# Two interleaved attention and MLP layers: residual rows and the probability spread issued from SyncE, and softmax's second half one PV step sooner

## The chip, the cores and the metric

The kernel runs on one core of one Trainium2 chip. The metric is the device time of one execution in microseconds (us). A quoted time is the median of several executions. "Span" is the length of the profiled execution; events inside it are given in us from its start. For the kernel before, that was one more execution, of 1328.15 us, 3.5 us above the median of the timed ones; for every other kernel it is one of the timed ones. Kernels are compared only within the same rounds.

## The reference

Two identical layers run one after the other. A layer is a dilated sliding-window attention followed by an MLP over the tokens, each with a residual and a layernorm in front. Everything is in bf16, with S = 2048 tokens, D = 1024, 32 heads of 32, a window of W = 8 positions two apart, and F = 3584.

```python
def _A_ref(x, wqkv, wo):                       # attention
    q, k, v = ...                              # x @ wqkv, split in 32 heads of 32
    idx = pos[:, None] - arange(8)[None] * 2   # 8 earlier positions, two apart
    logits = einsum("bhsd,bhswd->bhsw", q, k[idx]) * scale     # masked where idx < 0
    attn = softmax(logits)
    return einsum("bhsw,bhswd->bhsd", attn, v[idx]) @ wo
def _B_ref(x, w1, b1, w2, b2):                 # MLP over the tokens
    u = gelu(einsum("bsd,sf->bdf", layernorm(x), w1) + b1)
    return (einsum("bdf,fs->bds", u, w2) + b2).transpose
x = A_x
for _ in range(2):
    x = x + _A_ref(layernorm(x), A_wqkv, A_wo)
    x = x + _B_ref(layernorm(x), B_w1, B_b1, B_w2, B_b2)
```

## The kernel before

Positions two apart never mix in the attention, so the tokens fall into two classes of 1024. Per layer the attention runs in four blocks (n = 0 to 3, two per class). VectorE multiplies q with shifted k (`T`), TensorE sums over the head's channels with a selection matrix (`sc`), and softmax follows on VectorE and ScalarE. The probabilities `Pb` are then needed on all partitions of a head, so they are written to DRAM (`pd`, 256 KB) and read back with every row repeated eight times (`pb`, two reads of 1 MB). This is the "spread". VectorE multiplies `pb` with shifted v (the PV step). TensorE never waits for all that as long as other matmuls (projections, pieces of the MLP) can be woven in between.

The parts that matter here (cuts marked with `...`):

```python
# softmax, second half: normalise, write to DRAM, read back spread
nc.vector.tensor_tensor(out=Pb[:], in0=L[:], in1=m4[:, 1:2, :].to_broadcast([P, W, TB]), op=ALU.mult)
base = self.pd(n)[0, 0]
dst = bass.AP(base.tensor, base.offset, [(W * TB, 4 * SB), (4 * SB * W * TB, CH), (1, W * TB)])
nc.gpsimd.dma_start(out=dst, in_=Pb[:].rearrange("p u t -> p (u t)"))
self.spread(n)
...
def spread(self, n):
    for hf in range(2):
        pb = pbp.tile([P, 4, W, TB], BF16, name="pb", tag="pb")       # two buffers in all
        base = self.pd(n)[4 * hf, 0]
        src = bass.AP(base.tensor, base.offset, [(4 * SB * W * TB, CH), (0, P // CH), (1, 4 * W * TB)])
        nc.gpsimd.dma_start(out=pb[:].rearrange("p b u t -> p (b u t)"), in_=src)
...
# weights: all from SyncE
nc.sync.dma_start(out=t, in_=src)                                     # wq, wv: 512 KB each
...
# residual rows, 256 KB each
nc.gpsimd.dma_start(out=xrs[-1][:], in_=res[len(xrs) - 1])            # xr, for the output projection
nc.gpsimd.dma_start(out=xs[:], in_=src[c][i * P:(i + 1) * P, :])      # xs, for the second matmul of the MLP
...
nc.gpsimd.dma_start(out=dst_v[i], in_=xn[:])                          # xa, the attention's result, written
```

## Time and profile before

| | |
|---|---|
| time | 1324.73 us, median of 3 (1324.02 to 1324.88) |
| TensorE busy | 1275.1 of 1326.4 us |
| idle gaps of TensorE of over 0.3 us, summed | 40.0 us |
| stretches at half clock after such gaps | 30.6 us long, so some 15 us lost |
| `pb` read, issue to landing | 11.9 us (median of 16) |

These lines are from the page of the kernel before: busy time by engine, the granted TensorE clock in 40 slices of the span (tenths of full speed), the two DMA queues that matter (q0 is GpSimd's, q1 SyncE's; packets, MB, share of the DMA engines' time), and three kinds of transfer (count, KB each, median us to landing).

```profile
PE 1275.1 (96%) x6164; PEld 577.1 (44%) x6284; DVE 683.5 (52%) x861; ACT 439.8 (33%) x740; POOL 95.7 (7%) x230
...
PEclk9998999999999999999998999999899999999999
...
q1 hardware_dynamic: 224432, 116.67, 32.8%
q0 software_dynamic: 14368, 54.29, 14.6%
...
pb<-pd POOLq DMA_DIRECT2D x16, 1024.0 KB, 11.9
...
xs<-xa POOLq DMA_DIRECT2D x32, 256.0 KB, 3.7
wv<-in_A_wqkv_dram SPq DMA_DIRECT2D x14, 512.0 KB, 6.5
```

TensorE is busy 96% of the time, so only its gaps can be won. What ended its waits (the list of waits of TensorE before: us in total, times, longest):

```profile
PE sc L444 <- DVE T L439: 10.8, 4, 5.0
PE ps L622 <- DVE oT L506: 9.5, 3, 6.3
PE ps L681 <- DVE xo L686: 7.2, 1, 7.2
PE ps L622 <- DMA wo<-in_A_wo_dram: 3.4, 2, 2.9
PE ps L655 <- DVE xn L628: 2.1, 1, 2.1
```

With the letters that the prediction uses: A (102 us into the span, 5.0 us) and B (213 us, 4.4 us) are in the first line, C (301 to 303 us, 3.1 us) and F (946 us, 6.3 us) make the second, E (717 us, 7.2 us) is the third, H (197 us, 2.9 us) is in the fourth, D (340 us, 2.1 us) is the fifth. E is worth a look, because the change aims at it: the `xs` rows were issued at 704.8 us, behind the spread in GpSimd's program, and took 11.4 us (the instructions of tile `xs`, before, in this window; the issue line has count, duration, first and last start):

```profile
L672 POOL DMA_DIRECT2D xs<-xa x2: 543/547/551, 704.8 to 718.6; - x2
...
DMA to landing us min/median/max: 4.1/7.8/11.4
```

The weight load `wv` at 132.6 us lands in 3.7 us, though the spread of block 1 was issued 0.8 us after it, at 133.4 us (tiles `wv` and `pb`, before, 125 to 150 us):

```profile
L387 SPq DMA_DIRECT2D wv<-in_A_wqkv_dram x1: 368/368/368, 132.6 to 132.6; - x1
...
DMA to landing us min/median/max: 3.7/3.7/3.7
```

```profile
L482 POOL DMA_DIRECT2D pb<-pd x2: 513/513/513, 133.4 to 133.9; - x2
```

### The profile page before, as it was taken

What the parts mean: (1) busy time and instruction counts of PE and PEld (TensorE: products, weight loads), DVE (VectorE), ACT (ScalarE), POOL (GpSimd) and SP (SyncE); (2) the same over time, 40 slices, a digit from 0 to 9 for tenths busy, and PEclk for the clock granted to TensorE, in tenths of its full rate; (3) what the DMA queues carried; (4) which work ended last, traced back from release to release, by engine and by line L of the source; (5) the groups of instructions that cost most, each with busy time, mean ns of one, the idle gap of its engine ahead of it and who ended that gap; (6) DMA issues with size and microseconds to landing.
All of it is one profiled execution on the core that took longest, in us unless ns stands there. A gap on an engine that the chain in (4) does not pass through costs nothing.

```text
span 1326.4 us, 15310 instructions
## 1 busy us (share of the span) xinstructions
PE 1275.1 (96%) x6164; PEld 577.1 (44%) x6284; DVE 683.5 (52%) x861; ACT 439.8 (33%) x740; POOL 95.7 (7%) x230
## 2 busy tenths in 40 slices
PE   8999998999999999999997999999799999999999
PEld 4343433443444444444443444444344444444444
DVE  6879998989102323234796734878950033111111
ACT  6844445731313420024434424475122144000000
POOL 3000000101000000000001010011010000000000
PEclk9998999999999999999998999999899999999999
DMA  9751545553432248864658662438162232334331
GB/s 256 168 125 56 128 114 140 168 145 96 132 87 74 74 139 215 214 171 117 159 158 223 196 176 64 95 108 234 44 202 64 70 90 72 117 95 137 118 117 60
DMA packets 239448, 173.00 MB, mean 130 GB/s; under 512 B 32208, under 2 KB 227152, under 8 KB 237328
## 3 DMA queue, kind: packets, MB, share of 16 engines
q1 hardware_dynamic: 224432, 116.67, 32.8%
q0 software_dynamic: 14368, 54.29, 14.6%
q8 instruction: 49, 0.80, 0.3%
q10 hardware_dynamic: 576, 1.05, 0.2%
q14 instruction: 23, 0.19, 0.0%
HBM read 146.81 MB, written 18.87 MB: 125 GB/s over the span
## 4 chain that ended last, share of the span: by engine, by line
PE 64%; DVE 6%; DMA 4%; issue 1%; ACT 0%; POOL 0%; DVEq 0%
PE ps L681 27%; PE ps L655 22%; PE ps L409 11%; PE ps L622 3%; DVE pr L500 2%; DVE pr L504 1%; PE sc L444 1%; DMA xs<-xa 1%; DMA wq<-in_A_wqkv_dram 1%; DMA pb<-pd 1%; DMA xa<-xn 1%; DMA hT<-hb 0%; DVE xn L628 0%; DVE T L439 0%; DVE xn L625 0%
## 5 line engine op out<-in xcount | busy, mean ns | idle before, releaser
L681 PE MATMUL ps<-g,w 128*128 128x512 bf16 (+1 forms) x1786 | 389.8, 377 | 9.4 <-DVE xo L686 7.2
L655 PE MATMUL ps<-h,w 128*128 128x512 bf16 x1758 | 388.1, 380 | 5.3 <-DVE xn L628 2.1
L681 PEld LDWEIGHTS <-w 128*128 128x128 bf16 x1820 | 178.1, 98 | 219.4 <-issue 13.3
L655 PEld LDWEIGHTS <-w 128*128 128x128 bf16 x1792 | 175.8, 98 | 217.0 <-issue 7.2
L409 PE MATMUL ps<-hT,wq 128*128 128x512 bf16 (+1 forms) x1084 | 241.7, 376 | 4.6 <-DMA hT<-hb 1.6
L686 DVE SCALAR_TENSOR_TENSOR xo<-ps,b_sb,xs 128x512 bf16<-128x512 f32 (+1 forms) x65 | 45.6, 737 | 255.2 <-PE ps L681 239.6
L666 DVE TENSOR_TENSOR tmp<-ps,g 128x512 f32<-128x512 f32 x80 | 55.3, 692 | 229.0 <-PE ps L655 225.9
L439 DVE TENSOR_TENSOR T<-q,k 128x4096 bf16<-128x4096 bf16 x60 | 136.0, 2287 | 65.2 <-ACT q L413 55.5
L409 PEld LDWEIGHTS <-wq 128*128 128x128 bf16 x1112 | 108.8, 100 | 133.5 <-issue 13.6
L504 DVE TENSOR_TENSOR pr<-pr 128x2048 bf16<-128x2048 bf16 (+1 forms) x128 | 119.2, 947 | 0.1
L622 PE MATMUL ps<-wo,oT 128*128 128x512 bf16 x375 | 92.3, 384 | 13.7 <-DVE oT L506 9.5
L409 PE MATMUL ps<-hT,wv 128*128 128x512 bf16 x436 | 102.2, 384 | 0.9 <-issue 0.4
L416 ACT CAST k<-ps 128x1024 bf16<-128x1024 f32 x60 | 60.8, 1016 | 77.8 <-PE ps L409 76.5
L500 DVE TENSOR_TENSOR pr<-pb,v 128x2048 bf16<-128x2048 bf16 x64 | 75.8, 1214 | 19.4 <-DMA pb<-pd 15.4
L667 ACT ACTIVATE g<-tmp,b_sb 128x512 bf16<-128x512 f32 x80 | 57.7, 721 | 82.1 <-DVE tmp L666 82.1
L500 DVE TENSOR_TENSOR pr<-pb,g 128x2048 bf16<-128x2048 bf16 x64 | 76.2, 1214 | 11.1 <-DMA pb<-pd 11.1
L409 PEld LDWEIGHTS <-wv 128*128 128x128 bf16 x448 | 48.8, 112 | 51.8 <-issue 8.7
L661 ACT CAST g<-ps 128x512 bf16<-128x512 f32 x80 | 45.6, 589 | 70.3 <-PE ps L655 66.8
L192 ACT ACTIVATE ln<-mv,eps 128x1 f32<-128x1 f32 x37 | 10.9, 294 | 165.0 <-DVE mv L201 157.4
L622 PEld LDWEIGHTS <-oT 128*128 128x128 bf16 x384 | 37.2, 99 | 62.8 <-DVE oT L506 10.7
L413 ACT CAST q<-ps 128x512 bf16<-128x512 f32 x60 | 35.0, 585 | 52.3 <-PE ps L409 51.2
L416 ACT CAST g<-ps 128x1024 bf16<-128x1024 f32 x36 | 36.5, 1017 | 41.1 <-PE ps L409 41.1
(94 smaller groups left out, 633.8 us busy)
## 6 DMA issues: line engine op xcount, KB each, us to landing
w<-in_B_w_dram SPq DMA_DIRECT2D x96, 448.0 KB, 3.7
w<-in_B_w_dram SPq DMA_DIRECT2D x56, 512.0 KB, 4.3
wq<-in_A_wqkv_dram SPq DMA_DIRECT2D x38, 512.0 KB, 4.0
pb<-pd POOLq DMA_DIRECT2D x16, 1024.0 KB, 11.9
wo<-in_A_wo_dram SPq DMA_DIRECT2D x16, 512.0 KB, 4.0
xa<-xn POOLq DMA_DIRECT2D x32, 256.0 KB, 3.4
xs<-xa POOLq DMA_DIRECT2D x32, 256.0 KB, 3.7
wv<-in_A_wqkv_dram SPq DMA_DIRECT2D x14, 512.0 KB, 6.5
```

What stands on the lines that cost most here:

```text
L409: nc.tensor.matmul(ps[:, lo:hi], lhsT=cols, rhs=self.hT[c][hf][:, kt, lo:hi], start=(kt == 0), stop=(kt == KD - 1))
L416: nc.scalar.copy(out=window(buf, 0, PADK + hf * HT, [(KW + 1, 2), (1, HT)]), in_=ps[:].unsqueeze(1).to_broadcast([P, 2, HT]))
L439: nc.vector.tensor_tensor(out=T[:], in0=q.unsqueeze(1).to_broadcast([P, 4, SC]), in1=window(k, par, 2, [(2, 4), (1, SC)]), op=ALU.mult)
L500: nc.vector.tensor_tensor(out=pr[:, :, u, :], in0=pb[:, :, u, :], in1=window(self.v_of(c, dt), par, 2 + hf * HT, [(TB, 4), (2, 4), (1, TB) ...
L504: nc.vector.tensor_tensor(out=pr[:, :, 0:wd, :], in0=pr[:, :, 0:wd, :], in1=pr[:, :, wd:2 * wd, :], op=ALU.add)
L622: nc.tensor.matmul(ps[:], lhsT=at_.oT[c][kt][:, i * P:(i + 1) * P], rhs=wo_t[n][kt // 4][:, kt % 4, :], start=(kt == 0), stop=(kt == KD - 1))
L655: nc.tensor.matmul(ps[:], lhsT=wt[c][:, i, fl * P:(fl + 1) * P], rhs=h2[c][i // 4][:, i % 4, dc * 512:(dc + 1) * 512], start=(k == 0), sto ...
L661: nc.scalar.copy(out=gs, in_=ps[:])
L666: nc.vector.tensor_tensor(out=tmp[:], in0=ps[:], in1=gs, op=ALU.add)
L667: nc.scalar.activation(out=gs, in_=tmp[:], func=ACT.Gelu_apprx_tanh, bias=b1_sb[:, ft:ft + 1])
L681: nc.tensor.matmul(ps[:, 0:xc.stop - xc.start], lhsT=w2t[n][:, ft % HF, c::DIL], rhs=g[ft // GF][:, ft % GF, xc], start=(ft == 0), stop=(f ...
L686: nc.vector.scalar_tensor_tensor(out=xo[:, xc], in0=ps[:, 0:xc.stop - xc.start], scalar=b2_sb[:, i, c:c + 1], in1=xs[:, xc], op0=ALU.add, ...
```

## The change

The intent: GpSimd issues the spread, the residual rows and the result writes, and each waits behind the others in its program. Taking the rows and the spread to SyncE should free the `xa` writes (gap B) and the rows (gap E), and bring the spread forward a little. Softmax's second half is put ahead of one PV unit, so that `Pb` is ready sooner. The diff, complete but for context lines:

```diff
-            nc.gpsimd.dma_start(out=dst, in_=Pb[:].rearrange("p u t -> p (u t)"))
+            nc.sync.dma_start(out=dst, in_=Pb[:].rearrange("p u t -> p (u t)"))
             self.spread(n)
...
-                nc.gpsimd.dma_start(out=pb[:].rearrange("p b u t -> p (b u t)"), in_=src)
-        def pv(self, n, half, hf):
+                nc.sync.dma_start(out=pb[:].rearrange("p b u t -> p (b u t)"), in_=src)
+        def pv(self, n, half, hf, dqs=(0, 1)):
...
-            for dq in (2 * half, 2 * half + 1):
+            for dq in (2 * half + x for x in dqs):
...
                     if pv:
-                        yield from self.pv(n - 1, half, 0)
+                        yield from self.pv(n - 1, half, 0, (0,))
                     if half:
                         yield from self.softmax_back(n)
                     if pv:
+                        yield from self.pv(n - 1, half, 0, (1,))
                         yield from self.pv(n - 1, half, 1)
...
-                nc.gpsimd.dma_start(out=xrs[-1][:], in_=res[len(xrs) - 1])
+                nc.sync.dma_start(out=xrs[-1][:], in_=res[len(xrs) - 1])
...
-        nc.gpsimd.dma_start(out=xs[:], in_=src[c][i * P:(i + 1) * P, :])
+        nc.sync.dma_start(out=xs[:], in_=src[c][i * P:(i + 1) * P, :])
```

Below, "spread" means the `pd` and `pb` lines, "rows" the `xr` and `xs` lines, "order" the softmax lines.

## The prediction

> **What bounds it now.** TensorE. Page: PE 1275.1 of 1326.4 us busy; the chain of waits is 64% PE. What can be won is PE's idle time: gaps in the timeline add up to 40 us, and the clock record falls to 0.5 for 3.4 or 6.8 us after most gaps of over about 2 us (101, 213, 302, 340, 715, 944 us), another 15 us. By the wait list and the chain:
> - A, 102 us, 5.0: products T late, VectorE having idled 7.1 us for pb<-pd
> - H, 197 us, 2.9: wo landed 6.3 us after issue
> - B, 213 us, 4.4: VectorE waited 5.0 us for xa<-xn, behind the spread (+10.9 us)
> - C/D, 301-340 us, 5.3: last PV, then xa<-xn
> - E, 717 us, 7.2: xs<-xa, behind the spread on GpSimd's queue (+11.5 us)
> - F, 946 us, 6.3: last spread (pd 4.4 us, pb 8.3 us), then PV.
>
> **What the change does.** Issues leave GpSimd for SyncE, so xr, xs and both spread legs share one in-order queue with the weights.
>
> *Cheaper.* Per spread: no 0.3 us wake-up of GpSimd per leg, slightly earlier first byte (packet records: 1.2 us after issue for GpSimd's, 1.0 for SyncE's): 1 to 1.5 us. The rate should stay: the two pb reads (2.1 MB) take about 10.5 us, in 8 KB packets of 0.55 us, which no issuer changes. xa writes no longer stand behind pb: B's wait mostly goes.
>
> *Softmax.* The instruction order shows that Pb moves by only about one VectorE instruction (1.1 us), as the scheduler interleaved it already; only the last block moves by five (3.4 us). In each layer one group of 8 matmuls (1.7 us of filling) slips behind the output projection, so C and F must win more than that.
>
> *Dearer.* The Trainium skill, "DMA: Bandwidth & Descriptors", section "Queues, rings and completion order", says a ring is consumed in order while different rings alternate by packet. The trace agrees: xr issued behind pb on GpSimd's queue lands with it (+12.3 us), while a weight load on SyncE's queue got through in 6.7 us. Weights issued behind pb will now wait for all of it. By landing against first use: the wv load at 132.6 us (slack 3.9 us) lands some 7 us later and stalls PE about 4 us; the wq load at 639.6 us (slack 1.1 us) lands near 652 us and stalls PE 4.7 us, each with half-clock after. Later gaps (H, B; E) absorb part.
>
> **Sum.** First attention: A, H, B cost 17 us with clock; A shrinks 1, H and B go, the wv stall adds 6; C/D give 2-3: gain 6. Second layer, to 780 us: E shrinks to about 2, the wq stall costs as much: gain 0. To 980 us: Pb 3.4 + transfers 1.5-2 earlier, less 1.7, F falls to about 2.5 with half the clock loss: gain 5. Both MLPs: none.
>
> Predicted **1314 us**, range 1303 to 1325. Chances: faster by over 2% 0.06, within 2% 0.91, slower by over 2% 0.03.
>
> **Right or wrong.** pb still 7 and 11-12 us to landing; B gone, xa near 3-5 us; new PE waits on wv near 140 us and wq near 650 us; F under 3 us; 340-575 and 980-1320 us unchanged.
>
> **What would break it.** pb faster from SyncE (smaller packets): 1300. pd on fewer engines from SyncE, its outer dimension being 8: pd slower. In-order waits of SyncE holding up weights that I counted as free: 1335.

## More of the kernel before

`T` of the products and `pr` of PV share one pool of two buffers (`tpl`).

## The result, and the profile after

| | before | after |
|---|---|---|
| time, median us (lowest to highest; 4 runs each, same rounds) | 1324.67 (1324.02 to 1324.88) | 1328.48 (1327.61 to 1329.74) |
| ratio | | 1.0030, 95% interval 1.0013 to 1.0048 |
| span of the profiled run, mean granted clock | 1326.4, 0.988 | 1328.0, 0.987 |
| idle gaps of TensorE of over 0.3 us, summed | 40.0 | 40.1 |
| half-clock stretches, summed | 30.6 | 34.0 |

A ratio is the mean time of one kernel's runs over the mean of the other's runs of the same rounds, so it is not quite the ratio of the medians. The change is within 2%, and slightly slower: the time lies above the predicted range of 1303 to 1325 us.

The page after, the same lines as before:

```profile
PE 1276.9 (96%) x6164; PEld 577.2 (43%) x6284; DVE 682.6 (51%) x861; ACT 440.2 (33%) x740; POOL 47.3 (4%) x142
...
PEclk9998999999999999999899999999899999999999
...
q1 hardware_dynamic: 237040, 152.33, 42.7%
q0 software_dynamic: 5792, 18.63, 3.8%
...
pb<-pd SPq DMA_DIRECT2D x16, 1024.0 KB, 11.7
...
xs<-xa SPq DMA_DIRECT2D x32, 256.0 KB, 3.9
wv<-in_A_wqkv_dram SPq DMA_DIRECT2D x14, 512.0 KB, 5.5
```

36 MB moved from one queue to the other, GpSimd lost half its work, and `pb` takes as long as it did. TensorE's waits after:

```profile
PE sc L444 <- DVE T L439: 8.6, 3, 4.4
PE ps L623 <- DVE oT L506: 7.6, 3, 3.8
PE ps L409 <- DMA wq<-in_A_wqkv_dram: 5.5, 1, 5.5
PE ps L409 <- DMA wv<-in_A_wqkv_dram: 5.1, 1, 5.1
PE ps L682 <- DVE xo L687: 4.9, 1, 4.9
PE ps L656 <- ACT h L230: 2.4, 3, 1.8
PE ps L623 <- DMA wo<-in_A_wo_dram: 2.0, 2, 1.4
```

The four waits that were longest before all shrank, and two new ones came, both for weights and both single events: `wv` (TensorE idle until 145.4 us) and `wq` (until 652.7 us). The 1.8 us of `h` at 912 us is new as well.

The sum of gaps hides where the time changes. A better ledger is when TensorE first uses a given weight tile. The order of TensorE's weight tiles is the same in both kernels, so the same tile marks the same progress. These are worked out from the trace; "after" is the difference to before, and a change between two columns is what that stretch cost or won. Each row is one execution. As that of the kernel before was a slow one, the ledger flatters the others, this one by 2.2 us: it ends at +1.6 us, where the medians differ by 3.8:

```text
mark (tile first used)   wv     wo     w1     w1     wq     wq     wq     wq     wo     w1     w2
before, us            129.6  191.7  247.5  346.3  574.5  639.2  699.4  734.3  867.1  977.5 1307.5
after, difference      -0.2   +6.3   +3.0   +0.1   +0.1   -0.3   +6.9   +3.8   +2.3   +1.6   +1.6
```

The `wv` stall costs 6.5 us between 130 and 192 us: the gap of 5.1 and a half-clock stretch of 3.4 us. (The Trainium skill, "TensorE: Matmul & The Clock Gate", section "Part 1: The HAM clock gate", has TensorE fall to half rate after an idle window of about 3.4 us. The records here agree in kind, with stretches at 0.5 of 3.4 or 6.8 us, but shorter gaps are followed by one too: before, the gap of 2.1 us at 340 us is, and that of 2.9 us at 197 us is not.) The smaller H and B give back 3.3 us by 247 us, and C/D 2.9 by 346 us: the first attention ends at zero. The `wq` stall costs 7.2 us by 699 us, E gives back 3.1, and by the end 1.6 us are lost.

The first stall, seen from the load (tile `wv`, after; no landing time is recorded for this load):

```profile
L387 SPq DMA_DIRECT2D wv<-in_A_wqkv_dram x1: 369/369/369, 132.3 to 132.3; - x1
its engine sat idle before it (us, times) until:
  DMA wv<-in_A_wqkv_dram: 10.7, 2
```

It was issued as early as before (132.3 against 132.6 us), but the spread was issued at 130.8 us, ahead of it, in place of 133.4. Two lines from VectorE's waits after show what the stalls do next. In the kernel before, the same two lines stand at 26.6 and 0.3 us:

```profile
DVE pr L500 <- DMA pb<-pd: 18.6, 4, 6.5
...
DVE pr L500 <- PE sc L444: 12.0, 3, 6.3
```

VectorE cannot start a PV step because `pr` needs one of the two `tpl` buffers, and these are freed by matmuls that stand in TensorE's order behind the stalled one. So a stall of TensorE also stops VectorE, and the VectorE work that should have caught up by gaps H, B and E is late as well. (Below, the second of these waits is 7.1 us in e3, which has the `wv` stall, and absent in e6, which is e3 without it.)

### The profile page after: what moved, and what is told of

The parts are those of the page before. It is cut to its first block, busy times and chain, and to the rows that moved or that the text cites. A ratio compares the mean times of both kernels' runs of the same rounds, so it can differ in the third digit from the quotient of the medians.

```text
span 1328.0 us, 15358 instructions
## 1 busy us (share of the span) xinstructions
PE 1276.9 (96%) x6164; PEld 577.2 (43%) x6284; DVE 682.6 (51%) x861; ACT 440.2 (33%) x740; POOL 47.3 (4%) x142
## 4 chain that ended last, share of the span: by engine, by line
PE 75%; DVE 14%; DMA 8%; issue 2%; ACT 0%; POOL 0%; SPq 0%; DVEq 0%
PE ps L682 27%; PE ps L656 23%; PE ps L409 17%; PE ps L623 7%; DVE pr L500 4%; DVE pr L504 3%; PE sc L444 2%; DMA pb<-pd 2%; DVE T L439 2%; DMA pd<-Pb 1%; DMA wv<-in_A_wqkv_dram 1%; DMA wq<-in_A_wqkv_dram 1%; DMA xs<-xa 1%; DMA xr<-in_A_x_dram 1%; DMA g<-in_A_x_dram 1%
## 6 DMA issues: line engine op xcount, KB each, us to landing
pb<-pd SPq DMA_DIRECT2D x16, 1024.0 KB, 11.7
```

## The experiments

The prediction put the stalls down to the in-order ring, that is, the list of transfers that one issuing engine keeps: weights on SyncE's queue behind `pb` on the same queue. That is theory Q here. Its rival was that the order and timing of the issues do the harm, whichever ring they use; each expectation below names the theories as they stood when it was written. Before the runs, two tries to give weights more room (one more `wqp` or `wbp` buffer) and one to give VectorE more room (a third `tpl` buffer) did not build, because SBUF is full; so the coupling of VectorE to TensorE was not tested by itself.

For every run that kept the order of TensorE's weight tiles, this is the ledger of the profiled run against that of the kernel before (same marks as above). The runs are explained in turn below.

```text
mark                     wv     wo     w1     w1     wq     wq     wq     wq     wo     w1     w2
before, us            129.6  191.7  247.5  346.3  574.5  639.2  699.4  734.3  867.1  977.5 1307.5
after                  -0.2   +6.3   +3.0   +0.1   +0.1   -0.3   +6.9   +3.8   +2.3   +1.6   +1.6
e1_spread_only         -1.8   +6.8   +1.7   -2.0   -2.0   -2.2   +4.6   -5.1   -5.1   -6.6   -6.6
e2_rows_only           +0.2   +0.1   +2.3   -1.1   -1.1   -1.4   -1.4   -6.0   -7.5   -9.2   -9.2
e3_order_only          -0.1   +8.4   +7.0   +6.1   +6.1   +6.0   +6.0   +6.4   +5.9   +5.5   +5.5
e4_after_pb_pool       +0.2   +6.8   -0.6   -2.9   -2.9   -3.3   +4.4   +0.7   -0.6   -1.0   -1.0
e5_no_order            -0.7   +7.9   +4.3   +0.8   +0.8   +0.4   +6.6   +2.9   +1.5   +1.2   +1.2
e6_order_held          -1.1   -0.0   -0.5   -2.3   -2.3   -2.5   -2.5   -2.7   -3.3   -3.6   -3.6
e7_pool_held           +1.6   +2.4   -4.9   -6.0   -6.0   -6.4   +1.5   -6.3   -7.7   -9.4   -9.4
e8_order_2k            -0.3   -0.4   -3.7   -4.4   -4.4   -4.6   -4.6   -4.8   -5.5   -6.4   -6.4
e9_pool_held2          -0.9   -0.0   -7.3   -9.1   -9.1   -9.5   -9.5  -14.9  -16.3  -18.0  -18.0
e10_rows_2k            -0.6   -0.7   -2.0   -2.9   -2.9   -3.2   -3.2  -10.7  -11.7  -12.1  -12.1
e11_pool_2k            +1.2   +1.1   -6.1   -8.0   -8.0   -8.3   -8.3  -16.0  -17.2  -17.4  -17.4
e12_xs_pool            -0.9   +7.2   +4.3   +2.1   +2.1   +1.7   +8.8   -0.1   -0.5   -2.7   -2.7
e14_after_2k           -1.2   +3.7   +0.3   -5.2   -5.2   -5.6   +1.0   -2.5   -3.5   -4.3   -4.3
e15_pool_4k            -0.6   +5.5   +0.1   -1.3   -1.3   -1.8   -1.8   -6.5   -7.5   -9.7   -9.7
```

### The parts alone: e1, e2, e3, and the ring undone: e4

e1_spread_only is the kernel before with the spread from SyncE:

```diff
-nc.gpsimd.dma_start(out=dst, in_=Pb...)          # pd
+nc.sync.dma_start(out=dst, in_=Pb...)
-nc.gpsimd.dma_start(out=pb..., in_=src)
+nc.sync.dma_start(out=pb..., in_=src)
```

> Before, with only the two legs of the spread (pd<-Pb and pb<-pd) issued from SyncE; row loads and softmax order as before. Theory Q (weights issued behind pb on the same in-order ring wait for all of it): TensorE stalls of about 5 us on wv near 145 us and on wq near 650 us, wv then lands 11 to 13 us after its issue and not 3.7. The row loads on GpSimd's queue no longer stand behind pb, so the gaps near 213 us (xa) and 717 us (xs) shrink to under 2 us. Time 1320 to 1329 us, gains and stalls nearly cancelling. Rival S (what loses is the softmax order, 1.7 us of filling per layer): no such stall, time under 1318 us. Rival R (row loads on SyncE hold up the weights): no such stall here, under 1318 us.

Measured: 1321.75 us (1321.54 to 1324.66), ratio 0.9980 (0.9969 to 0.9992). Both weight stalls are there (6.8 and 5.3 us), and E is gone.

e2_rows_only is the kernel before with the rows from SyncE:

```diff
-nc.gpsimd.dma_start(out=xrs[-1][:], in_=...)     # and xs in the same way
+nc.sync.dma_start(out=xrs[-1][:], in_=...)
```

> Before, with only the row loads xr and xs issued from SyncE. Theory Q: wv near 132 us still lands within 4 us and wq near 640 us within 7 us, no stall at 145 or 650 us; the gap at 717 us goes under 3 us because xs no longer queues behind pb; the one near 213 us stays over 3 us because xa still does. Time 1313 to 1320 us. Rival R: waits of SyncE for row buffers hold up weight loads, new TensorE waits on weights of over 3 us in sum, time 1326 us or more. Rival S says as Q.

Measured: 1318.94 us (1315.92 to 1320.52), ratio 0.9952 (0.9939 to 0.9965). No weight stall; E fell from 7.2 to 3.5 us, not quite under the 3 that I expected.

e3_order_only is the kernel before with the softmax lines of the diff alone:

```diff
-    yield from self.pv(n - 1, half, 0)
+    yield from self.pv(n - 1, half, 0, (0,))
     ... softmax_back(n)
+    yield from self.pv(n - 1, half, 0, (1,))
```

> Before, with only the softmax's second half one PV step sooner; all DMAs as before. Theory Q: nearly nothing, the two gaps before the output projections change by the 1.7 us of filling that slips behind them less what Pb wins (about 1 us at 303 us, 3 us at 946 us): 1322 to 1327 us. Rival S: 1328 us or more, the loss of the whole change.

Measured: 1333.24 us (1331.53 to 1333.65), ratio 1.0059 (1.0047 to 1.0071). This is the first surprise: the `wv` stall is there (5.9 us until 146.4 us) although `pb` is on GpSimd's ring. The time is the one that rival S named, but not for its reason: 8.5 us are lost by the mark at 192 us, where the load stalls, and the filling that slips makes a gap of only 1.76 us (916 us). The load took 13.8 us (tile `wv` of e3, 125 to 150 us):

```profile
L387 SPq DMA_DIRECT2D wv<-in_A_wqkv_dram x1: 368/368/368, 132.5 to 132.5; - x1
...
DMA to landing us min/median/max: 13.8/13.8/13.8
```

e4_after_pb_pool is the whole change with `pb` alone put back on GpSimd:

```diff
-nc.sync.dma_start(out=pb..., in_=src)
+nc.gpsimd.dma_start(out=pb..., in_=src)
```

> The changed kernel with one line put back: pb<-pd from GpSimd's queue again, pd<-Pb, row loads and softmax order as changed. Theory Q: both stalls (5.1 us on wv at 145 us, 5.5 us on wq at 653 us) go, as do the VectorE waits for the qk matmuls behind them (5.3 and 6.3 us); the gap near 717 us goes under 2 us, the one near 213 us is back at 3 us or more since xa stands behind pb again. Time 1309 to 1318 us. Rival S or R: within 3 us of the changed kernel's 1328.

Measured: 1327.21 us (1322.92 to 1329.68), ratio 1.0013 (0.9998 to 1.0028). Both stalls stay (5.3 and 6.5 us), E stays at 4.2 us, and B goes; all four against theory Q's forecast. It falls as the whole explanation: a weight load is starved on the other ring too.

How a load is starved there is seen by counting packets. The Trainium skill ("DMA: Bandwidth & Descriptors", section "Queues, rings and completion order") says that one engine takes its rings in turn, a whole packet at a time, and each ring in order. Both halves of that can be seen here, each in one kernel. These are the packets of the DMA engines while `pb` and `wq` compete: first the kernel after, from 641 to 648 us (one ring), then e4, from 640 to 648 us (two rings); columns are packets, MB, share of 16 engines' time:

```profile
DMA packets 208, 1.57 MB, mean 225 GB/s; under 512 B 16, under 2 KB 16, under 8 KB 16
...
q1 hardware_dynamic: 208, 1.57, 103.8%
```

```profile
DMA packets 448, 1.82 MB, mean 227 GB/s; under 512 B 16, under 2 KB 240, under 8 KB 240
...
q0 software_dynamic: 224, 1.70, 94.2%
q1 hardware_dynamic: 224, 0.11, 9.0%
```

In one ring, practically nothing but 8 KB packets of `pb` passes, and `wq` comes after it. In two rings the turns are exactly even, 224 packets to 224. But a packet of `pb` is 8 KB and one of `wq` is 512 B, so the load that TensorE needs gets 0.11 of 1.82 MB: 28 packets per us, where it gets over 500 per us when it is alone (567 in the microsecond from 651 us of the trace after). Even turns between unequal packets starve the small ones nearly as well as a queue does.

That makes theory R (race): what decides is which of the two is first. In the kernel before, `wv` won by 0.8 us and landed in 3.7 us. `wq` was issued 0.2 us before `pb`, at 639.6 us, and landed in 6.7. In e3 and after, the `pb` that meets `wv` is 1 to 3 us earlier and the load is not, so the load loses.

A lead in issue alone is not enough, though. In e4 and e7 `wq` was issued first too, by 0.08 and 0.06 us, and stalled all the same (timeline of e4, SyncE and GpSimd, 636 to 637.5 us; start and duration in us):

```profile
636.35 0.37 SPq L387 DMA_DIRECT2D wq<-in_A_wqkv_dram  x1
636.43 1.07 POOL L482 DMA_DIRECT2D pb<-pd  x2 [19.80 <-DMA pd<-Pb]
```

With leads of 0.17, 0.15 and 0.18 us (before, e6, e3) it got through, in 6.7, 7.7 and 4.6 us. The load is 1024 packets of 512 B. When the first packet of `pb` came, 605 and 617 of them had passed in e4 and e7, and 820, 817 and 890 in the other three. So what counts, it seems, is how much of the load has passed by then, as the rest has to take turns with 8 KB packets.

### Is it a race? e6, e7 and e9 hold `pb` back

If so, issuing `pb` *later* in the blocks concerned must make the kernel faster. To be free of races of the other kind, the hold is real work: two copies of `Pb` onto itself on GpSimd, which wait for the `pd` write and stand before `pb` in GpSimd's program. The values do not change. e6_order_held is e3 with:

```diff
+if (self.li, n) in ((0, 1), (1, 4)):
+    for _ in range(2):
+        nc.gpsimd.tensor_copy(out=Pb[:], in_=Pb[:])
 self.spread(n)
```

> The softmax order alone (1333.2 us measured, with the wv stall of 5.9 us at 146 us though pb is on GpSimd's ring), and in two blocks (first layer n=1, second layer n=4) GpSimd makes two in-place copies of Pb (values unchanged) between pd and pb, so that pb is issued some 2 to 4 us later, after the wv load. Theory R: the wv load is then issued first and lands in 3.5 to 7 us, the stall near 146 us is gone (under 1 us), and the time falls by 5 to 9 us to 1324 to 1328, although pb comes later. Theory L (the order itself puts the weight load late, pb has nothing to do with it; or a later pb makes VectorE later): the stall stays at 4 us or more and the time is 1333 or more.

Measured: 1325.00 us (1322.76 to 1329.00), ratio 1.0001 (0.9985 to 1.0017). The stall is gone. The load and the spread in e6 (tiles `wv` and `pb`, 125 to 150 us):

```profile
L387 SPq DMA_DIRECT2D wv<-in_A_wqkv_dram x1: 368/368/368, 131.5 to 131.5; - x1
...
DMA to landing us min/median/max: 4.0/4.0/4.0
```

```profile
L485 POOL DMA_DIRECT2D pb<-pd x2: 510/512/513, 135.3 to 136.8; - x2
```

The wait, 13.8 us in e3, is 4.0 us here, and a later `pb` made the kernel some 8 us faster (0.6% between the two ratios). The ledger shows more. e3 is behind e6 by 8.4 us at the mark at 192 us, and by 8.4 at 346, 8.5 at 639 and 9.1 at the end. **Nothing later absorbed this stall.**

e7_pool_held is e4 with the same hold:

> The whole change with pb back on GpSimd's ring (1327.2 us measured, stalls of 5.3 us on wv at 146 us and 6.5 us on wq at 651 us), with the same hold of pb in the two blocks. Theory R: wv issued before pb and both stalls gone (each under 1.5 us), time down by 8 to 14 us to 1313 to 1319. Theory L: both stalls stay, 1326 or more. If only one goes, about 1321.

Measured: 1318.79 us (1318.52 to 1319.80), ratio 0.9953 (0.9940 to 0.9967). The `wv` stall is gone, the `wq` stall stayed (6.2 us). The reason is a mistake of mine: the blocks of a layer are n = 0 to 3, so the second hold named a block that does not exist. The one that competes with `wq` is n = 0 of the second layer, where `wq` had the lead of 0.06 us seen above. Within one run, the held block lost its stall and the unheld one kept it. e9_pool_held2 puts it right:

```diff
-if (self.li, n) in ((0, 1), (1, 4)):
+if (self.li, n) in ((0, 1), (1, 0)):
```

> As the run e7 (the whole change, pb back on GpSimd's ring, two blocks' pb held back by two in-place copies on GpSimd), with the second hold put on the right block: in e7 it sat on the second layer's n=4, which is not the block at 633 us; that is n=0 of the second layer, and the wq stall of 6.2 us at 647 us stayed there while the held wv stall went. Theory R: now both stalls are gone (each under 1.5 us), wv and wq land within 8 us of issue, and the time falls from 1318.8 to 1309 to 1314. If the wq stall stays over 4 us although its load is issued over 1 us before pb, the theory falls for that load.

Measured: 1316.41 us (1310.16 to 1317.89), ratio 0.9911 (0.9889 to 0.9933). In the profiled run (1310.16 us) both stalls are gone; at the mark at 699 us it is 11.0 us ahead of e7, of which it had 3.1 before the block. The median missed my 1309 to 1314: the six runs were 1310.2, 1310.7, 1316.2, 1316.6, 1317.1 and 1317.9. The profile shows one of the two good ones. Another race that is still a near tie, won in two runs and lost in four, would look like this: in the profiled run `xs` and `pb` were issued at 690.85 and 690.98 us. I have no profile of a slower run, so that cause is argued, not shown.

### Where the whole differs from its parts: e5 and e12

Spread alone wins 0.2%, rows alone win 0.5%, and the whole loses 0.3%. Is the order to blame? e5_no_order is the whole change without the softmax lines.

> The whole change without the softmax part: xr, xs and both legs of the spread issued from SyncE, PV and softmax in the order of before. Theory R (race between rings: what decides is whether the 8 KB packets of pb or the weight load start first; each part that brings pb a microsecond sooner loses that race): order adds its own loss of 1.7 us of filling per layer, so without it 1317 to 1321 us, ratio 0.994 to 0.997; the wv stall near 145 us stays (pb is issued before wv in SyncE's own order) and the wq stall near 650 us too, E gone. Theory A (the parts add: spread -3, rows -6.4, against the 1328 of the whole, order +8): 1315 to 1317 us. If instead it is over 1325 us, order is not what makes the whole lose, and SyncE's shared ring is.

Measured: 1328.82 us (1327.77 to 1329.83), ratio 1.0028 (1.0014 to 1.0042). Neither of my two figures came true, and E, expected gone, is 4.2 us: without the order the rest loses as much as the whole. So inside the whole, the order costs nothing measurable, because the stall that it provokes alone is there anyway. And the two halves that win alone undo each other. The ledger says where. Between 699 and 734 us, gap E, e1 wins 9.7 us and e2 wins 4.6, but e5 wins 3.7 and after 3.1. In e1 the spread is on SyncE and `xs` on GpSimd, so `xs` no longer stands behind the spread's waits. In the whole both are on SyncE, and `xs` stands behind `pb` again, as it did on GpSimd before (tile `xs`, after, 695 to 722 us):

```profile
L673 SPq DMA_DIRECT2D xs<-xa x1: 1048/1048/1048, 709.3 to 709.3; - x1
...
DMA to landing us min/median/max: 11.5/11.5/11.5
```

e12_xs_pool is the whole change with `xs` alone back on GpSimd:

```diff
-nc.sync.dma_start(out=xs[:], in_=src[c][i * P:(i + 1) * P, :])
+nc.gpsimd.dma_start(out=xs[:], in_=src[c][i * P:(i + 1) * P, :])
```

> The whole change with xs alone back on GpSimd. In the spread alone E was gone because xs was issued from GpSimd at 694 us, before the spread, while in the whole change it stands behind pb in SyncE's program and was issued at 709 us and landed 11.5 us later. Theory O (what xs gains depends on not sharing an issuing engine with pb; the two halves of the change undo each other): xs issued some 10 us sooner and E, 4.9 us in the whole change, gone (under 1 us); both weight stalls stay (5 us each); time 1320 to 1324. If E stays over 3 us, xs was late for another reason.

Measured: 1325.37 us (1320.11 to 1327.03), ratio 0.9986 (0.9967 to 1.0005); a little above my range of 1320 to 1324, which its six runs straddle. The step itself is as expected (tile `xs`, e12):

```profile
L673 POOL DMA_DIRECT2D xs<-xa x1: 537/537/537, 697.9 to 697.9; - x1
...
DMA to landing us min/median/max: 4.0/4.0/4.0
```

`xs` goes 11 us sooner, E falls to 0.7 us, and the stretch from 699 to 734 us wins 8.9 us in place of 3.1. What the rows gain depends on *not* sharing an issuing engine with the spread, and the change moved both. Gap B shows the same on a smaller scale: VectorE's wait of 5.0 us for the `xa` write went, and a wait of 3.1 us for `xr`, now behind `pb` on SyncE, took its place (VectorE's waits after, 205 to 222 us):

```profile
DVE xn L626 <- DMA xr<-in_A_x_dram: 3.1, 1, 3.1
```

### Smaller packets: e8, e10, e11, e14, e15 and e13

If turns are even by packet, smaller packets of `pb` leave more for the others. In e8_order_2k each `pb` read of e3 is cut into four reads of one block each, with contiguous runs of 2 KB in place of 8. The same edit makes e10_rows_2k out of e2, e11_pool_2k out of e4 and e14_after_2k out of the whole change (there from SyncE):

```diff
-base = self.pd(n)[4 * hf, 0]
-src = bass.AP(base.tensor, base.offset, [(4 * SB * W * TB, CH), (0, P // CH), (1, 4 * W * TB)])
-nc.gpsimd.dma_start(out=pb[:].rearrange("p b u t -> p (b u t)"), in_=src)
+for b in range(4):
+    base = self.pd(n)[4 * hf + b, 0]
+    src = bass.AP(base.tensor, base.offset, [(4 * SB * W * TB, CH), (0, P // CH), (1, W * TB)])
+    nc.gpsimd.dma_start(out=pb[:, b:b + 1].rearrange("p b u t -> p (b u t)"), in_=src)
```

> The softmax order alone, with each pb read cut into four DMAs of 2 KB packets in place of one of 8 KB (same bytes, still on GpSimd's ring, eight issues of about 0.53 us in place of two). Theory R with alternation by packet: against 2 KB packets of about 0.14 us a weight load of 1 KB packets caught in the middle gets about four times its former 25 packets per us, so wv lands in 5 to 9 us in place of 13.8 and the stall near 146 us falls from 5.9 to under 2 us; time 1324 to 1329. If the DMA engines share by bytes or the ring behind it is simply blocked, wv still lands in 12 us or more and the stall stays over 4 us. pb itself should land in 9 to 14 us; if that grows over 14, the later pb hides the verdict in the total and only the landing of wv counts.

Measured: 1321.94 us (1320.98 to 1328.72), ratio 0.9986 (0.9966 to 1.0007). No `wv` stall; the load landed in 6.2 us though it was issued 0.4 us after the first piece of `pb`. The time is better than I expected. All of the 2.8 us that e8 ends ahead of e6 in the ledger are won from 192 to 247 us. The two gaps there are about as long in both (2.3 and 2.8 us in e8, 2.3 and 2.9 in e6), but after each e6 has a half-clock stretch of 3.4 us and e8 has none, so that lead is mostly one of clock. The spread is hardly faster over all eight blocks (median 12.1 us from its first issue, against 12.9 in the kernel before). The trace records the pieces on GpSimd's ring as packets of 4 KB, not of 2 KB as I had written.

> xr and xs from SyncE (1318.9 us measured), and each pb read in four DMAs of 2 KB packets, on GpSimd's ring; softmax order of before. Theory R: no stall on wv or wq (as in the rows alone, where the loads won by under 1 us), the xs load at 699 us, which started with pb and landed in 12.1 us there, lands in under 9 us, E falls from 3.5 us to about 1, and A, which waits for pb, stays at 4 to 5.5 us. Time 1312 to 1317. If the smaller packets do nothing to loads that already win, 1318 to 1320.

Measured: 1316.60 us (1315.03 to 1318.16), ratio 0.9925 (0.9909 to 0.9941). `xs` at 697.1 us landed in 5.5 us in place of 12.1, and E fell from 3.5 to 2.2 us (about 1 expected). The gain over e2 is 0.3% between the two ratios, and their intervals just touch.

> The whole change, but pb back on GpSimd's ring and in 2 KB packets. With 8 KB packets it took 1327.2 us, with both stalls (5.3 and 6.5 us). Theory R: both stalls under 1.5 us without any hold, wv and wq landing in 5 to 9 us, E under 3 us; time 1309 to 1315, best so far. If wq stays at 10 us and more, 1318 or more.

Measured: 1312.07 us (1310.68 to 1312.61), ratio 0.9888 (0.9873 to 0.9903). This is the best kernel, 1.1% below before and 1.4% below after by the two ratios, and its runs lie close together. TensorE's longest waits in e11 have neither `wv` nor `wq` in them (`wo` is a weight too, and was waited for before):

```profile
PE ps L624 <- DVE oT L507: 9.7, 3, 4.6
PE sc L444 <- DVE T L439: 7.9, 4, 6.5
PE ps L657 <- ACT h L230: 2.4, 3, 1.8
PE ps L624 <- DMA wo<-in_A_wo_dram: 2.4, 2, 1.8
PE ps L683 <- DVE xo L688: 2.0, 1, 2.0
```

Two things were open then, and three more runs went to them: does the cut help by smaller packets, or by the openings that eight issues of half a microsecond leave between the pieces; and does sharing SyncE's ring cost anything of its own?

e14_after_2k, the whole change with the pieces on SyncE's ring:

> The whole change with each pb read in four pieces as in e11, but on SyncE's ring as the change has it. Theory F (within one ring in order): wv and wq are issued behind eight issues, some 3 us later than in the whole change, and land only after the last pb piece: over 11 us after the first pb issue; stalls of 5 to 8 us stay, 1325 to 1332. If the two stalls are under 2 us and the time is 1316 or less, sharing the ring costs nothing and packet size was all.

Measured: 1325.53 us (1323.14 to 1329.57), ratio 1.0007 (0.9991 to 1.0024). Both stalls stay, 3.3 and 4.8 us, below the 5 to 8 expected. In order within the ring is real: no 512 B packet of `wq` shows in the trace before 642 us, 8.4 us after the first piece of `pb` was issued and with the last ones still passing. So the shared ring, which e4 showed not to be needed for the stalls, does cause them by itself: the small packets that let a load issued later through on the other ring (e8, e11) left both stalls on this one. Against e11 the ring (with the issues that go with it) is worth 1.2%.

e15_pool_4k is e11 with two pieces per read in place of four (runs of 4 KB):

> As e11 with two pieces per pb read in place of four (runs of 4 KB, four issues). Theory P: if the packets come out at 4 KB, as in e11, the same result, 1310 to 1316, both stalls under 2 us; if they come out at 8 KB (a packet holding two runs, as the 4 KB packets of e11 suggest), both stalls stay and the time is 1322 to 1328. Theory S: half the spacing, stalls about half, 1316 to 1321, whatever the packets are.

Measured: 1317.60 us (1315.85 to 1323.13), ratio 0.9952 (0.9934 to 0.9971). The packets are 4 KB, as in e11, and yet the `wv` stall is there (4.6 us); the `wq` load won its race, issued 0.1 us before `pb`. The turns are near even again (e15, 138 to 143 us), at about 50 packets per us for each side, twice the 28 of e4, as packets of half the size should give:

```profile
q0 software_dynamic: 248, 0.92, 78.2%
q1 hardware_dynamic: 278, 0.27, 24.9%
```

In e11, by contrast, the trace shows GpSimd's ring nearly empty just as `wv` came: 12 and 30 packets of `pb` in the two microseconds from 137 us, and 198 and 263 of `wv`. So theory P (packet size) is right about the rates, but at 4 KB its rate alone is not enough to save `wv`; that the openings between the pieces (theory S) did it in e11 fits these counts, but was not tested by itself. The time of e15 lies in theory S's range (1316 to 1321 us) and outside P's, but S had both stalls at about half, and one is 4.6 us and the other gone.

e13_pool_8x8k was to separate them cleanly: eight issues as in e11, each over a quarter of the partitions with whole 8 KB runs.

```diff
+for q in range(4):
+    base = self.pd(n)[4 * hf + 4 * SB * (CH // 4) * q, 0]
+    src = bass.AP(base.tensor, base.offset, [(4 * SB * W * TB, CH // 4), (0, P // CH), (1, 4 * W * TB)])
+    nc.gpsimd.dma_start(out=pb[32 * q:32 * q + 32].rearrange("p b u t -> p (b u t)"), in_=src)
```

> As e11 (the whole change, pb on GpSimd's ring in eight issues; 1312.1 us, no stalls), but each of the eight pieces takes a quarter of the partitions with whole 8 KB runs, in place of all partitions with 2 KB runs (recorded there as packets of 4 KB). Number of issues, their spacing and the bytes are the same. Theory P (packet size): the packets are 8 KB again, the weight load gets some 25 packets per us, both stalls come back (over 4 us each), 1322 to 1328. Theory S (spacing: the issues leave openings): no stall over 1.5 us and 1310 to 1316.

Measured: 1332.05 us (1331.26 to 1334.06), ratio 1.0058 (1.0046 to 1.0070). It is no control, though. The build put TensorE's instructions in another order than e4's, which it did not for e11 and e15, and A is gone while other gaps are new. The `wv` load was issued at 125.9 us, 10 us before that block's `pb`. The run decides nothing, and how much of e11's gain is packet size and how much is openings stays open.

## Why the prediction was wrong

What it had right:

- TensorE bounds the kernel and only its gaps count: busy time moved by 1.8 us, about what 3.4 us more of half clock cost.
- The rate of `pb` does not depend on the issuer: 11.7 us (7 landings recorded of 16) against 11.9.
- Both new stalls, their places and about their sizes: "some 4 us" on `wv` near 140 us and 4.7 us on `wq` near 650 us were 5.1 and 5.5 us, with half clock after.
- The order moves `Pb` of the last block by 3.2 us against the work around it (905.2 us in place of 906.1, with the ledger 2.3 us behind; 3.4 predicted), and costs one group of filling: the new gap of 1.76 us at 912 us appears in the runs with the order and is not among the gaps of those without it.

What failed is the sum, in these terms:

- **"Later gaps (H, B; E) absorb part."** H and B do not: e3 against e6 carries the whole `wv` stall, 8.4 us, from 192 us to the end. E gave back at most a part: e7 lost 7.9 us to e9 by the `wq` stall, and 5.5 of them remain from 734 us on (not a clean pair, as `xs` was issued 0.7 us ahead of `pb` in e7 and 0.1 in e9). A stall stops VectorE too, through the shared buffers, so the work whose lateness makes the later gaps is pushed out with it; this is read from VectorE's waits and was not tested by itself.
- **"H and B go"** was worth some 9 us with clock in the first attention. The stretch with both gave 3.3 us: H fell from 2.9 to 1.4, B only from 4.4 to 2.6, because `xr` now waits behind `pb` on SyncE as `xa` had on GpSimd. With the stall at 6.5 us, the predicted gain of 6 was a loss of 0.1 (the mark at 346 us).
- **"E shrinks to about 2"** was 4.9, for the same reason: `xs` stayed behind `pb`, as e12 shows. With the `wq` stall at 7.2 us in the ledger, "gain 0" by 780 us was a loss of 2.2 (from 346 to 867 us).
- **"F ... gain 5"** was 0.7 from 867 to 978 us: the gap shrank from 6.3 to 3.8, but the filling took 1.8 back, and the transfers were not the 1.5 to 2 us faster that I had counted (`pb` was issued 5.3 us after `pd`, as against 4.7 before).

These terms predicted 6 + 0 + 5 = 11 us of gain and measured -0.1 - 2.2 + 0.7 = -1.6, which is the ledger's last column. The medians say -3.8. The other 2.2 us come from the profiled runs, which lie 3.5 us (before) and 1.3 us (after) above their medians; where in those runs, the traces do not show.

The mechanism was half right. Loads behind `pb` in the same ring do wait for nearly all of it (after, e14). But I took another ring for safe, from a load that got through in 6.7 us; that load had been issued 0.2 us ahead of `pb`. The kernel before was not safe but lucky by 0.2 and 0.8 us, so a part that advances the spread can break it, even the order alone with no DMA moved (at `wv`).

Why the whole is worse than its parts: by the ratios, the parts alone sum to -0.20 - 0.48 + 0.59 = -0.09%, and the whole is at +0.30%, so some 5 us are lost. (The ledger gives 11.9 us, which is too much, because its slow run of the kernel before counts once in the whole and three times in the parts.) Two stretches of the ledger stand out, with opposite signs. The `wv` stall costs 17.0 us in the parts together, as e1 and e3 both have it, and 6.5 in the whole: it is lost only once. E's stretch wins 13.9 us in the parts together and 3.1 in the whole: it can be won once, by parting `xs` from `pb`, and moving both wins little of it.

## What to carry to other kernels

Before moving a large transfer to another queue or forward in time, list the small urgent loads that are issued within a microsecond or two of it, on every queue, and see who is first and by how much: against 8 KB packets a lead of 0.15 us was enough here and one of 0.08 was not. A load with small packets that comes second to 8 KB packets is starved whichever ring it is on. Moving two things that wait on each other from one in-order issuer to another in-order issuer moves the wait with them: part them, do not carry them along. A large read on its own ring, cut into pieces with small packets, let others through here (e8, e11; in part in e15). Do not count on later gaps to absorb a whole stall if the stalled engine holds buffers that the other engine needs.

## What the Trainium skill lacked or had wrong

- "DMA: Bandwidth & Descriptors", section "Queues, rings and completion order": the turns by packet are right (224 to 224 here), but the page does not say what follows for unequal packets. 512 B packets against 8 KB packets got 28 per us, against over 500 alone, and the 512 KB load of e3, in packets of 1 KB, took 13.8 us in place of 4.0 (e6). Its section "SWDGE vs HWDGE vs iDMA" calls a packet of at most 4096 B preferable and the packet the boundary at which an engine switches, but does not draw this consequence.
- The same page, "Rules for kernel authors", advises to coalesce and to use at least 1 MiB per DMA for bandwidth. Here 1 MB reads cut into four of 256 KB made the kernel faster by 1.2% (e11 against e4, from the two ratios), when others were waiting on another ring; cut in the same way on the ring of those others (e14) there was no clear gain. The rule needs that exception.
- The same page, "Issuing engine by pattern", calls HWDGE generally faster. For this read there was no clear difference: 11.7 us from SyncE (the 7 of 16 whose landing is recorded), 11.9 from GpSimd.
- The same page, "Issuing engines are not separate DMA queues", says that more issuing engines only save issue time, usually small. Here a waiting issue held up those behind it: `xs` went out 11 us sooner when it had another issuer than `pb` (e12).
- No page says for this chip how runs become packets, beyond the preferred 4096 B above: runs of 2 KB were recorded as packets of 4 KB from GpSimd (e11) and of 2 KB from SyncE (e14), runs of 8 KB as 8 KB from both.
